# Neighbour rows of v copied in two blocks of 23 chunks instead of one of 47, with other numbers for the transfers in the plan and a new order

## The chip, the cores and the metric

The kernel runs on one core of one Trainium2 chip. Five instruction queues work beside each other: PE (TensorE, the matrix unit), DVE (VectorE), ACT (ScalarE), POOL (GpSimd) and SP (SyncE, which here only starts transfers). Each queue is executed strictly in order, and queues wait for each other by semaphores. Sixteen DMA engines move data between memory and the on-chip buffers. The metric is the device time of one execution in microseconds (us). Of each kernel several executions are timed; the median is quoted. One further execution is recorded by the hardware profiler, and all rows below come from such a recording.

## The reference

Chunked attention over 4 batches, 8 heads, 768 rows and head size 64. Each chunk of 32 queries sees its own 32 keys, 16 to the left, 8 to the right and 8 memory rows. Its output is laid out as 3072 tokens of 512 and goes into a noisy top-2 router over 8 experts, each of them two matrix products with a relu between.

```python
for c in range(S // 32):                      # 24 chunks
    l_start, r_end = max(0, c*32 - 16), min(S, c*32 + 32 + 8)
    k_full = concatenate([mem_k, k[:, :, l_start:r_end]], axis=2)
    v_full = concatenate([mem_v, v[:, :, l_start:r_end]], axis=2)
    a = softmax(q[:, :, c*32:c*32+32] @ k_full.T / sqrt(64))
    out[:, :, c*32:c*32+32] = a @ v_full
...
x = out.transpose(0, 2, 1, 3).reshape(3072, 512)
noisy = x @ w_gate + log1p(exp(x @ w_noise)) * noise
top2 = the two largest of each row of noisy, with their softmax as weights
for e in range(8):                            # w1[e] 512x1024, w2[e] 1024x512
    rows = tokens that chose e
    y[rows] += weight[rows] * (relu(x[rows] @ w1[e]) @ w2[e])
```

## The kernel before, in words

**Who decides the order.** The program isn't written in the order in which it runs. A planner (class `Planner`, L65 to L203) gets a list of operations. Each has a label, the engines it may run on with an assumed duration, the operations it depends on, the buffers it takes, a priority, and, where it starts a transfer, a pair `dma=(transfer, latency)`. `run` (L109) walks through time: of the operations that could start on an engine within 0.25 us of the earliest, it takes the one with the lowest priority number. It also picks the engine for operations that two could do. The instructions are then emitted in the order of the planned starts, and the hardware keeps to that order on each queue. Nothing of the plan's times is enforced on the chip; only the order and the choice of engine remain. Three things steer it: the durations, the table `SHIFT`, which adds to the priority of a label (or of its n-th operation, "label#n"), and `FETCH`, which describes pauses that the plan assumes for PE when it passes a multiple of 128 products (block, first edge, pause before a time, that time, pause behind it).

**Attention.** The work is cut into 16 pairs of heads (n = 0 to 15), 8 groups (g) of two pairs, and 4 batches (b) of four pairs. For each group the POOL queue loads q and k (`lq`, `lk`, L504, three buffers each) and v in two halves (`lv`, L513). A half of v holds two heads side by side as 48 chunks: for each chunk the 32 rows of the chunk itself stand on partitions 16 to 47 of the half's 64 partitions (three buffers, vg0 to vg2). Three kinds of small transfers on the SP queue fill the other partitions: the memory rows (`lm`, L524, out of `memv`, a part of the buffer XS that the experts use later), the 16 rows to the left (`spread`, L530, from the preceding chunk) and the 8 rows to the right (L531, from the following chunk). They copy within the buffer, over all 48 chunks of a half at once. The rows copied from one head into the other's edge are harmless: the scores there are masked.

Per pair there follow on PE, DVE and ACT: transposes of q and k (`tq`, `tk`, L551), their copies out (`eq`, `ek`, L367 and L369), scores (`sc`, L574 to L581), maximum (`mx`, L588), subtraction (`sb`, L604), exponential (`ex`, L607), transposes of the result (`tp`, L613) and their copy, the product with v (`pvo`, L627, 24 products; it needs `lm` and both halves' copies), reciprocal of the sums (`rc`, L631), multiplication into the row buffer of the batch (`ml`, L643), transposes of the rows (`tx`, L652).

**Ranking.** When a batch's four pairs are done, its 768 tokens are routed: logits (`lg`, L689), noise (`r1`, L695), choice of two experts (`r2`, L703 to L718, VectorE), running counts (`r3`, PE), a place in the experts' lists (`r3s` L745 and L747, `r6` L765 to L768), one-hot tables (`r8` L740, `r8a` L782), their product (`r9`, L789) and from it the indices by which the gathers fetch tokens (L798, L803, L816 in `tab`). The weights of the two experts come from `r4` (L755) and `r7` (L899 to L903). Tokens beyond a list's capacity are handled by `s0` to `s3` (L840 to L864). The SP queue writes each batch's finished rows to memory (`rows`, L909): batches 0 and 1 whole (row buffers xrow0 and xrow1), batches 2 and 3 (xrow2, xrow0 again) in two parts, `rows_x` as soon as the batch's last `ml` is done and `rows_g` after `r7`.

**Experts.** Indirect gathers on the POOL queue (L945) fetch 128 tokens each; PE turns them (L976), and they are copied into XS (`xev`, L367 and L369). Then each expert's first product (L1051), relu (L1061), second product (L1092), weighting and adding (L1101 to L1111), and scatter to the output (L1123). The weights w1 (L923) and w2 (L925) are loaded on the POOL queue too. The first gathers need only the lists of batches 0 to 2 (index buffer `gid_s`), the others those of all batches.

Of the kernel before, what the change touches and what calls it, by code (L numbers as in the profile page):

```python
# [22 lines left out]
FETCH = (128, 94, 6.9, 97.0, 3.2)  # L23
SHIFT = {
# [40 lines left out]
class Planner:  # L65
# [43 lines left out]
    def run(self):  # L109
        free, dma_free, sync_free, lanes, paced, products, busy = {}, 0.0, 0.0, [], 0.0, 0, 0.0  # L110
# [96 lines left out]
def kernel(  # L207
# [14 lines left out]
    nc = tc.nc  # L222
# [20 lines left out]
    OW = D + 2  # L243
# [253 lines left out]
    for g in range(NG):  # L497
# [11 lines left out]
        def v_load(o, hh, bv=bv, g=g, h0=h0, b=b):  # L509
# [7 lines left out]
                 prio=pr + 2 + 0.5 * hh, dma=(1.6, 1.6), tag="attn") for hh in range(2)]  # L517
# [8 lines left out]
        lm = op("lm", ("SP", 0.4), mem_rows, deps=[c_mv] + zd, after=lv, use=[bv], prio=pr + 3, dma=(0.3, 1.8), tag="attn")  # L526

        def spread(o, hh, bv=bv):
            vt = bv.t[64 * hh:64 * hh + 64, hh]
            nc.sync.dma_start(out=vt[:left_ctx, 1:], in_=vt[chunk:chunk + left_ctx, :2 * ncnk - 1])  # L530
            nc.sync.dma_start(out=vt[left_ctx + chunk:WIN, :2 * ncnk - 1], in_=vt[left_ctx:left_ctx + right_ctx, 1:])  # L531

        ln = [op("ln", ("SP", 0.3), lambda o, hh=hh, f=spread: f(o, hh), deps=[lv[hh]], after=[lm] if hh else [], use=[bv], prio=pr + 3 + 0.2 * (hh + 1), dma=(0.5, 1.8), tag="attn") for hh in range(2)]
        groups.append((bq, bk, bv, lq, lk, [lm] + ln))

    xrows = {}
# [726 lines left out]
```

## Time and profile before

| What | Value |
|---|---|
| timed runs | 338.48, 338.59 and 340.06 us |
| median | 338.59 us |
| the profiled execution's own time | 337.19 us |
| its span, first to last instruction | 335.70 us |
| mean granted TensorE clock in the span | 0.911 |
| data moved in the span | 43.56 MB in 56205 packets, 130 GB/s |

The execution falls into four parts. Attention runs until about 88 us, with loads on the DMA engines nearly all the time. From there to 126.5 us the end of attention and the ranking of batches 2 and 3 run, with VectorE the busiest engine. The experts run from 126.5 to 328.4 us, with PE busy almost without a gap. The last 7.3 us are the last tile's way to memory.

In the rows, a group of instructions is named by its engine, its line, and what it writes and reads; "[0.57 <-PE ps_o L627]" says that the engine had been idle for 0.57 us and what ended it. "SPq" and "POOLq" are the instructions that start a transfer on those queues.

### The profile page before, as it was taken

The numbers are of one execution on the slowest core, as the hardware profiler recorded it, in microseconds if no ns is written. First come the engines' busy times: TensorE is split into PE (matmuls) and PEld (weight loads), VectorE is DVE, ScalarE is ACT, GpSimd is POOL, SyncE is SP. The second block draws the span as 40 slices with busy tenths as digits, with TensorE's granted clock in tenths as the row PEclk, the third lists the DMA queues.
The fourth block names the chain that finished last, engine by engine and source line by source line (L and its number), as shares of the span: only waits on it lengthen the run. The fifth ranks groups of instructions, "written<-read, shape, count | busy, mean of one in ns | idle before, by whom it ended". The sixth has DMA issues, their size and how long they took to land.

```text
span 335.7 us, 7347 instructions
## 1 busy us (share of the span) xinstructions
PE 277.1 (83%) x2955; PEld 173.2 (52%) x2972; DVE 161.1 (48%) x370; ACT 146.0 (43%) x262; POOL 122.5 (36%) x177
## 2 busy tenths in 40 slices
PE   0683575767475659999999999999999999999991
PEld 0672464656354546664555755544544644744540
DVE  7683568897689886383243134043034023042141
ACT  7484765865494333762421621602701713704400
POOL 7771430332000494889752301232032032042062
PEclk9998769896795557999999999999999999999996
DMA  7999999999994249748999984884613612022022
GB/s 102 204 150 145 162 164 158 158 220 136 149 224 128 88 114 159 144 137 163 173 189 232 240 148 94 117 152 103 111 53 72 103 54 80 2 83 79 0 109 92
DMA packets 56205, 43.56 MB, mean 130 GB/s; under 512 B 29613, under 2 KB 49070, under 8 KB 56166
## 3 DMA queue, kind: packets, MB, share of 16 engines
q0 software_dynamic: 50096, 36.40, 83.7%
q1 hardware_dynamic: 5782, 6.57, 9.4%
q8 instruction: 24, 0.39, 0.5%
q14 instruction: 15, 0.12, 0.1%
q10 hardware_dynamic: 288, 0.07, 0.1%
HBM read 56.54 MB, written 10.85 MB: 201 GB/s over the span
## 4 chain that ended last, share of the span: by engine, by line
PE 55%; DMA 18%; DVE 9%; issue 8%; POOL 4%; ACT 2%; POOLq 2%; SPq 0%; DVEq 0%; ACTq 0%
PE ps_l L1092 19%; PE ps_l L1051 17%; DMA vg<-in_v_dram 11%; PE ps_g L1051 6%; PE ps_g L1092 5%; DMA vg<-vg 5%; POOL out_dram L1123 2%; PE ps_q L551 2%; DMA qn<-in_q_dram 2%; PE ps_o L627 1%; PE ps_l L976 1%; POOLq L1179 1%; DVE mx L588 1%; PE ps_g L652 1%; DVE xrow L643 1%
## 5 line engine op out<-in xcount | busy, mean ns | idle before, releaser
L1092 PE MATMUL ps_l<-w2l,ht 128*128 128x512 bf16 x341 | 78.2, 379 | 0.6
L1061 ACT ACTIVATE ht<-ps_l 128x384 bf16<-128x384 f32 (+2 forms) x106 | 47.7, 488 | 59.6 <-PE ps_l L1051 57.1
L1092 PEld LDWEIGHTS <-ht 128*128 128x128 bf16 x448 | 43.6, 98 | 51.1
L1123 POOL DMA_INDIRECT out_dram<-acc,oid x28 | 28.8, 1028 | 87.8 <-DVE acc L1111 82.9
L1111 DVE SCALAR_TENSOR_TENSOR acc<-ps_l,gates,acc 128x512 f32<-128x512 f32 x26 | 19.5, 751 | 63.9 <-PE ps_l L1092 61.0
L1051 PEld LDWEIGHTS <-w1t 128*128 128x128 bf16 x416 | 31.2, 99 | 19.2 <-issue 1.4
L1051 PE MATMUL ps_l<-XS,w1t 128*128 128x384 bf16 (+4 forms) x316 | 39.7, 284 | 0.0
L1051 PEld LDWEIGHTS <-w1l 128*128 128x128 bf16 x320 | 29.8, 98 | 18.8
L1061 ACT ACTIVATE ht<-ps_g 128x384 bf16<-128x384 f32 (+2 forms) x41 | 18.7, 490 | 46.7 <-PE ps_g L1051 46.5
L1051 PE MATMUL ps_l<-XS,w1l 128*128 128x256 bf16 (+3 forms) x240 | 38.8, 314 | 0.0
L627 PE MATMUL ps_o<-vg,PT 128*32 128x132 bf16 x384 | 12.5, 284 | 18.0 <-DMA vg<-vg 15.7
L367 ACT COPY kT<-ps_q 64x768 bf16<-64x768 bf16 x28 | 22.2, 792 | 10.8 <-PE ps_q L551 10.5
L513 POOL DMA_DIRECT2D vg<-in_v_dram x16 | 15.3, 960 | 25.2 <-PE ps_o L627 22.4
L1092 PE MATMUL ps_g<-w2l,ht 128*128 128x512 bf16 x91 | 21.9, 379 | 0.3
L551 PE MATMUL ps_q<-identb,qn 128*64 128x128 bf16 x192 | 11.3, 273 | 10.5 <-DMA qn<-in_q_dram 9.9
L945 POOL DMA_INDIRECT xl<-x_rows,gid x16 | 16.6, 1037 | 8.4 <-DMA w1t<-in_moe_w_dram 4.6
L1103 DVE TENSOR_SCALAR acc<-ps_l,gates 128x512 f32<-128x512 f32 x14 | 10.5, 751 | 18.5 <-PE ps_l L1092 15.3
L627 PEld LDWEIGHTS <-PT 128*32 128x32 bf16 x384 | 8.5, 122 | 20.4 <-issue 18.8
L607 ACT ACTIVATE P<-sd 128x768 bf16<-128x768 f32 x16 | 13.5, 845 | 6.3 <-DVE sd L604 6.1
L588 DVE TENSOR_REDUCE mx<-ps_s 128x12 f32<-128x768 f32 x16 | 15.2, 952 | 1.1 <-PE ps_s L581 1.0
L604 DVE TENSOR_TENSOR sd<-ps_s,mx 128x768 f32<-128x768 f32 x16 | 15.3, 956 | 0.8
L643 DVE TENSOR_TENSOR xrow<-ps_o,rec 128x768 bf16<-128x768 f32 x16 | 15.3, 957 | 0.5
(178 smaller groups left out, 369.6 us busy)
## 6 DMA issues: line engine op xcount, KB each, us to landing
w2l<-in_moe_w_dram POOLq DMA_DIRECT2D x8, 1024.0 KB, 9.5
w1t<-in_moe_w_dram POOLq DMA_DIRECT2D x4, 1024.0 KB, 20.9
w1l<-in_moe_w_dram POOLq DMA_DIRECT2D x4, 1024.0 KB, 8.3
kn<-in_k_dram POOLq DMA_DIRECT2D x8, 384.0 KB, 13.5
qn<-in_q_dram POOLq DMA_DIRECT2D x8, 384.0 KB, 11.6
vg<-in_v_dram POOLq DMA_DIRECT2D x16, 192.0 KB, 16.3
x_rows<-xrow SPq DMA_DIRECT2D x2, 792.0 KB
vg<-vg SPq DMA_DIRECT2D x16, 96.9 KB
```

What stands on the lines that cost most here:

```text
L367: A.copy(dst, src)
L513: G_.dma_start(out=vt[p0:p0 + chunk, hh, :, :D], in_=bass.AP(v.tensor, v.offset + hd * S * D, [[D, chunk], [chunk * D, 2 * ncnk], [1, D]]))
L551: P_.transpose(out=dst.t[64 * hh:64 * hh + 64, t * QP:(t + 1) * QP], in_=s[:, j + 2 * hh, t, :], identity=identb)
L588: mx = op("mx", ("DVE", 0.98), lambda o, bmx=bmx, bS=bS: V.tensor_reduce(out=bmx.t, in_=sv(bS), axis=AX, op=Alu.max), deps=[sc], alloc=[bm ...
L627: P_.matmul(out=pvw[32 * r:32 * r + 32, u // UB, u % UB], lhsT=PT[:, u, 32 * r:32 * r + 32], rhs=vt[:, :, ncnk * j + c], start=True, stop= ...
L643: V.tensor_tensor(out=x5, in0=ov(bO)[:, :, :, :, :D], in1=r5.to_broadcast([128, 2, UB, 2, D]), op=Alu.mult)
L945: G_.indirect_dma_start(out=bx.t[:n], out_offset=None, in_=src, in_offset=bass.IndirectOffsetOnAxis(ap=ids_[:n, c:c + 1], axis=0), bounds_ ...
L1051: P_.matmul(out=dst, lhsT=w1b[e].t[:, kp, f * 128:(f + 1) * 128], rhs=src, start=(kp == 0), stop=(kp == KP - 1), skip_group_check=True)
L1061: A.activation(out=dst, in_=s_, func=Act.Relu)
L1092: P_.matmul(out=gy.t, lhsT=ht.t[:, f, j, :], rhs=w2b[e].t[:, f, :], start=(f == 0), stop=(f == FB - 1))
L1111: V.scalar_tensor_tensor(out=ba.t, in0=gy.t, scalar=gate, in1=ba.t, op0=Alu.mult, op1=Alu.add)
L1123: G_.indirect_dma_start(out=out_part[nv], out_offset=bass.IndirectOffsetOnAxis(ap=oid[:, c:c + 1], axis=0), in_=ba.t, in_offset=None, boun ...
```

## The change

The copies of the neighbour rows are written over two heads with 23 chunks each, where they were written over 47 chunks that include the seam between the heads. The row of 48 x 66 elements is split as two of 24 x 66; a copy then has two blocks of 23 x 66 = 1518 elements per partition where it had one of 47 x 66 = 3102. The chunk that was copied across the seam isn't copied any more.

Beside it, numbers that only the planner uses change: what a transfer on SP costs (`lm` 0.4 to 1.3, `ln` 0.3 to 1.25, and 1.8 to 4.0 us until a neighbour copy has landed), a load of v (1.6 to 1.7), the pauses of `FETCH`, and the time at which engines and transfers start (1.1 to 4.75 us, formerly 0). The table `SHIFT` is another one. And the copies of gathered tokens into XS get one more dependency: on the last group's memory rows, which are read from a part of XS.

```diff
-FETCH = (128, 94, 6.9, 97.0, 3.2)
+FETCH = (128, 94, 6.6, 100.0, 3.2)
 SHIFT = {
-    "c_mv": 79.0, "c_ones": 19.7, "c_smallv": 124.2, "c_wg": 14.0, "ek": 14.6, "ek#23": 6.3, "ek#29": 11.1, "ep": 38.1, "ep#3": 23.7, "eq":
...
+    "ek": 19.8, "ek#17": -24.3, "ek#19": -51.3, "ep#1": -28.0, "eq#1": 19.5, "ex": 33.6, "ex#4": -21.4, "exx": 53.8, "exx#7": -17.1, "fo":
...
     def run(self):
-        free, dma_free, sync_free, lanes, paced, products, busy = {}, 0.0, 0.0, [], 0.0, 0, 0.0
+        free, dma_free, sync_free, lanes, paced, products, busy = dict(POOL=1.6, DVE=1.1, ACT=1.1, SP=1.1, PE=1.1), 4.75, 4.75, [], 0.0, 0, 0.0
...
         lv = [op("lv", ("POOL", 1.05), ...
-                 prio=pr + 2 + 0.5 * hh, dma=(1.6, 1.6), tag="attn") for hh in range(2)]
+                 prio=pr + 2 + 0.5 * hh, dma=(1.7, 1.6), tag="attn") for hh in range(2)]
...
-        lm = op("lm", ("SP", 0.4), mem_rows, deps=[c_mv] + zd, after=lv, use=[bv], prio=pr + 3, dma=(0.3, 1.8), tag="attn")
+        lm = op("lm", ("SP", 1.3), mem_rows, deps=[c_mv] + zd, after=lv, use=[bv], prio=pr + 3, dma=(0.3, 1.8), tag="attn")
 
         def spread(o, hh, bv=bv):
-            vt = bv.t[64 * hh:64 * hh + 64, hh]
-            nc.sync.dma_start(out=vt[:left_ctx, 1:], in_=vt[chunk:chunk + left_ctx, :2 * ncnk - 1])
-            nc.sync.dma_start(out=vt[left_ctx + chunk:WIN, :2 * ncnk - 1], in_=vt[left_ctx:left_ctx + right_ctx, 1:])
-
-        ln = [op("ln", ("SP", 0.3), lambda o, hh=hh, f=spread: f(o, hh), ..., dma=(0.5, 1.8), tag="attn") for hh in range(2)]
+            vt = bv.t[64 * hh:64 * hh + 64, hh].rearrange("p (j c) d -> p j (c d)", j=2)
+            nc.sync.dma_start(out=vt[:left_ctx, :, OW:], in_=vt[chunk:chunk + left_ctx, :, :-OW])
+            nc.sync.dma_start(out=vt[left_ctx + chunk:WIN, :, :-OW], in_=vt[left_ctx:left_ctx + right_ctx, :, OW:])
+
+        ln = [op("ln", ("SP", 1.25), lambda o, hh=hh, f=spread: f(o, hh), ..., dma=(0.5, 4.0), tag="attn") for hh in range(2)]
...
-            ev = op("xev", ..., xev, deps=[tt], use=[gx], prio=prio)
+            ev = op("xev", ..., xev, deps=[tt, groups[-1][5][0]], use=[gx], prio=prio)
```

The new order, at three places. The first is the SP queue behind the copies of group 5 (buffer vg2_100 until the row write, then group 6 in vg0_98); before, the row write of batch 0 (xrow0_78) stands between the two halves of group 4 (vg1_99).

Before:

```order
L530 DMA vg1_99<-vg1_99 16x3102
L531 DMA vg1_99<-vg1_99 8x3102
L909 DMA x_rows<-xrow0_78 128x6x264
L524 DMA vg2_100<-XS_77 8x3168 x2
L530 DMA vg1_99<-vg1_99 16x3102
L531 DMA vg1_99<-vg1_99 8x3102
L524 DMA vg0_98<-XS_77 8x3168 x2
```

Of the change:

```order
L530 DMA vg2_100<-vg2_100 16x2x1518
L531 DMA vg2_100<-vg2_100 8x2x1518
L909 DMA x_rows<-xrow0_78 128x6x264
L530 DMA vg0_98<-vg0_98 16x2x1518
L531 DMA vg0_98<-vg0_98 8x2x1518
```

The row write has moved behind all copies of groups 4 and 5, and directly ahead of those of group 6. The shape 16x2x1518 in place of 16x3102 is the copy in two blocks.

The second place is the end of the SP queue, where the copies of the last group (vg1_99) and the row writes of batches 1 (xrow1_79), 2 (xrow2_80) and 3 (xrow0_78 again) stand. Before:

```order
L524 DMA vg1_99<-XS_77 8x3168 x2
L909 DMA x_rows<-xrow1_79 128x6x264
L530 DMA vg1_99<-vg1_99 16x3102
L531 DMA vg1_99<-vg1_99 8x3102
L909 DMA x_rows<-xrow2_80 128x6x256
L530 DMA vg1_99<-vg1_99 16x3102
L531 DMA vg1_99<-vg1_99 8x3102
L909 DMA x_rows<-xrow2_80 128x6x8
```

Of the change:

```order
L524 DMA vg1_99<-XS_77 8x3168 x2
L909 DMA x_rows<-xrow2_80 128x6x256
L530 DMA vg1_99<-vg1_99 16x2x1518
L531 DMA vg1_99<-vg1_99 8x2x1518
L530 DMA vg1_99<-vg1_99 16x2x1518
L531 DMA vg1_99<-vg1_99 8x2x1518
L909 DMA x_rows<-xrow1_79 128x6x264
L909 DMA x_rows<-xrow2_80 128x6x8
```

Batch 2's rows now stand ahead of both halves of the last group's copies, and batch 1's behind them.

The third place is VectorE's queue around the last two multiplications of attention (L643, of pairs 14 and 15, into xrow0_78; the later one is pair 15's, "ml15"). The other names there belong to batch 2: pos, at and slot are its places, fl and fs part of them, ohl its one-hot table, gid_s the indices of the first gathers, tab the running list. Before:

```order
L765 TENSOR_TENSOR pos_2127<-ps_g0_84,pk_2041 128x168
L767 TENSOR_REDUCE at_2128<-pos_2127 128x6
L768 TENSOR_TENSOR slot_2129<-at_2128,fs_2051 128x6
L782 TENSOR_TENSOR ohl_158<-ramp_132,slot_2129 128x768
L631 RECIPROCAL rec0_113<-ps_o0_121 128x12
L643 TENSOR_TENSOR xrow0_78<-ps_o0_121,rec0_113 128x6x2x64
L803 SCALAR_TENSOR_TENSOR gid_s_162<-ps_g1_85,tab_161 128x28
L798 SCALAR_TENSOR_TENSOR gid_s_162<-ps_g1_85,tab_161 64x2x2
L798 SCALAR_TENSOR_TENSOR gid_s_162<-ps_g1_85,tab_161 64x2
L816 TENSOR_TENSOR tab_161<-ps_g1_85,tab_161 128x28
L631 RECIPROCAL rec1_114<-ps_o0_121 128x12
L643 TENSOR_TENSOR xrow0_78<-ps_o0_121,rec1_114 128x6x2x64
```

Of the change:

```order
L631 RECIPROCAL rec1_114<-ps_o0_121 128x12
L643 TENSOR_TENSOR xrow0_78<-ps_o0_121,rec1_114 128x6x2x64
L864 TENSOR_TENSOR tab_161<-ps_g1_85,tab_161 32x1
L745 TENSOR_TENSOR fl_2188<-pk_2084,flip_140 128x168
L747 TENSOR_REDUCE fs_2189<-fl_2188 128x6
L765 TENSOR_TENSOR pos_2199<-ps_g0_84,pk_2084 128x168
L767 TENSOR_REDUCE at_2200<-pos_2199 128x6
L768 TENSOR_TENSOR slot_2201<-at_2200,fs_2189 128x6
L782 TENSOR_TENSOR ohl_158<-ramp_132,slot_2201 128x768
L774 SCALAR_TENSOR_TENSOR base3_151<-ps_g0_84,smin_139 128x28
L840 TENSOR_REDUCE cap_2208<-pk_2084 128x6
L841 TENSOR_SCALAR cap_2208<-cap_2208 128x6
```

Batch 2's places, its one-hot table and its indices stand behind ml15, where they stood ahead of it; the indices gid_s follow three rows further on.

More of the change, by code (lines that the diff above doesn't have):

```diff
@@ L524, in mem_rows @@
                 nc.sync.dma_start(out=bv.t[64 * hh + WIN:64 * hh + CTX, hh], in_=memv[64 * hh + n_mem * g:64 * hh + n_mem * (g + 1)])
-        lm = op("lm", ("SP", 0.4), mem_rows, deps=[c_mv] + zd, after=lv, use=[bv], prio=pr + 3, dma=(0.3, 1.8), tag="attn")
+        lm = op("lm", ("SP", 1.3), mem_rows, deps=[c_mv] + zd, after=lv, use=[bv], prio=pr + 3, dma=(0.3, 1.8), tag="attn")
         def spread(o, hh, bv=bv):
-            vt = bv.t[64 * hh:64 * hh + 64, hh]
-            nc.sync.dma_start(out=vt[:left_ctx, 1:], in_=vt[chunk:chunk + left_ctx, :2 * ncnk - 1])
-            nc.sync.dma_start(out=vt[left_ctx + chunk:WIN, :2 * ncnk - 1], in_=vt[left_ctx:left_ctx + right_ctx, 1:])
-        ln = [op("ln", ("SP", 0.3), lambda o, hh=hh, f=spread: f(o, hh), deps=[lv[hh]], after=[lm] if hh else [], use=[bv], prio=pr + 3 + 0.2 * (hh + 1), dma=(0.5, 1.8), tag="attn") for hh in range(2)]
+            vt = bv.t[64 * hh:64 * hh + 64, hh].rearrange("p (j c) d -> p j (c d)", j=2)
+            nc.sync.dma_start(out=vt[:left_ctx, :, OW:], in_=vt[chunk:chunk + left_ctx, :, :-OW])
+            nc.sync.dma_start(out=vt[left_ctx + chunk:WIN, :, :-OW], in_=vt[left_ctx:left_ctx + right_ctx, :, OW:])
+        ln = [op("ln", ("SP", 1.25), lambda o, hh=hh, f=spread: f(o, hh), deps=[lv[hh]], after=[lm] if hh else [], use=[bv], prio=pr + 3 + 0.2 * (hh + 1), dma=(0.5, 4.0), tag="attn") for hh in range(2)]
         groups.append((bq, bk, bv, lq, lk, [lm] + ln))
@@ L985, in turn_ops @@
             w = KP * m * 128
-            ev = op("xev", DA(0.2 + w / 1900, 0.2 + w / 1250), xev, deps=[tt], use=[gx], prio=prio)
+            ev = op("xev", DA(0.2 + w / 1900, 0.2 + w / 1250), xev, deps=[tt, groups[-1][5][0]], use=[gx], prio=prio)
             for ps, _ in units:
@@ L1003, in turn_ops @@
             d_ = 0.4 if half and len(ps) > 1 else 0.2
-            ev = op("xev_a" if half == 0 else "xev", ("ACT", 0.2 + w / 1250) if half == 0 else DA(d_ + w / 1900, d_ + w / 1250), xev, deps=[tt], use=[gx], prio=prio)
+            ev = op("xev_a" if half == 0 else "xev", ("ACT", 0.2 + w / 1250) if half == 0 else DA(d_ + w / 1900, d_ + w / 1250), xev, deps=[tt, groups[-1][5][0]], use=[gx], prio=prio)
             for p in ps:
```

26 rows, old and new, of the table SHIFT are left out of this document.

## The prediction

> **What bounds the kernel now.** I read the page first (busy shares, the granted clock, the DMA share), then a table of stages cut where the chain of waits changes its nature, then the chain itself.
>
> ```profile
> PE 277.1 (83%) x2955; PEld 173.2 (52%) x2972; DVE 161.1 (48%) x370; ACT 146.0 (43%) x262; POOL 122.5 (36%) x177
> PEclk9998769896795557999999999999999999999996
> DMA  7999999999994249748999984884613612022022
> ```
>
> DMA is at 9 tenths from the second slice to the twelfth (8.4 to about 100 us), and the TensorE clock drops in exactly that part. PE's 83% is therefore an average of two different kernels. The stage table tells them apart (columns: stretch, length, busy us of PE, PEld, DVE, ACT, POOL, granted clock, DMA share, GB/s).
>
> ```profile
> 0.00:31.50 31.50, 14.44 (x290) 12.34 (x290) 20.93 (x43) 20.29 (x20) 21.10 (x60) 0.98 1.70 152
> 31.50:88.50 57.00, 37.18 (x903) 29.58 (x903) 41.74 (x86) 36.26 (x52) 15.00 (x18) 0.80 2.05 163
> 88.50:126.50 38.00, 24.97 (x495) 20.86 (x495) 31.75 (x98) 18.62 (x30) 12.40 (x16) 0.63 0.71 139
> 126.50:150.50 24.00, 23.53 (x251) 16.11 (x251) 14.56 (x62) 14.05 (x50) 16.86 (x21) 0.94 0.76 151
> 150.50:328.40 177.90, 176.95 (x1019) 94.33 (x1034) 51.41 (x81) 56.73 (x111) 55.82 (x62) 1.00 0.55 113
> 328.40:335.70 7.30, 0.00 (x0) 0.00 (x0) 0.75 (x1) 0.00 (x0) 1.28 (x2) 0.65 0.20 69
> ```
>
> From 126.5 to 328.4 us, the expert stage, PE is busy 200.48 of 201.90 us: only 1.42 us can be won there. The last 7.3 us are the last scatter. So nearly all that this change can win or lose lies before 126.5 us, in attention and ranking. The chain there:
>
> ```profile
> 27.02 20.94 DMA vg<-in_v_dram
> 47.98 0.54 SPq L530
> 48.57 8.86 DMA vg<-vg
> 57.57 0.85 PE ps_o L627 x24
> ...
> 80.77 0.54 SPq L530
> 81.36 7.04 DMA vg<-vg
> 88.53 0.85 PE ps_o L627 x24
> ```
>
> Up to 88.5 us the end is set by loads of v, then by the neighbour copies (7.04 and 8.86 us from issue to release), then by the product with v (L627). The load at 27.02 takes 20.94 us because it stands behind the loads of q and k issued before it. Behind 88.5 us VectorE takes over (columns: stretch, length, busy us, clock, DMA share, GB/s):
>
> ```profile
> 88.50:93.80 5.30, 3.01 (x4) 0.70 1.62 164
> 93.80:104.00 10.20, 9.62 (x24) 0.90 1.04 219
> 104.00:114.80 10.80, 9.24 (x27) 0.50 0.16 44
> 114.80:126.50 11.70, 9.87 (x46) 0.50 0.52 146
> ```
>
> 28.73 busy of 32.7 us: from 93.8 us on what counts is in which order VectorE's queue stands, and whether the last v is there in time.
>
> **The copies.** Count of DMAs, partitions and source: unchanged, 32 copies. Bytes fall by one chunk of 48 per row and direction (3102 to 3036 elements, 2%), and the runs double, from one to two per row. The trace has no copy of two runs. Its nearest rows are the two landings above, 7.04 and 8.86 us for the same bytes: their difference, 1.82 us, bounds what a copy may gain or lose by its form; I take 0, since the bytes are nearly the same and the copies' time is mostly waiting beside the loads. The Trainium skill ("DMA: Bandwidth & Descriptors", section "Queues, rings and completion order") says that each DMA engine goes round the queues with work, one packet at a time. If the two runs are two packets, each copy waits for one more packet of the loads; no row here shows a packet's turn. By that rule the sum could only rise, within the same 1.82 us.
>
> **The plan's numbers** (durations of copies, start times, prefetch) cost nothing themselves: they choose the order. The added dependency of the late copies into XS on the last memory rows is no wait: on the SP queue those rows stand ahead of the last copies, which are issued by 99.78 us, and XS is first written at 122.78 us (both rows below).
>
> **Loads of q, k, v.** The POOL queue now builds the identity first and then starts q before k. The sixteen v loads and sixteen q and k loads stay on one queue, and the last two v loads still have all others and one w1 load ahead of them. While that queue is never empty, their landing depends on the amount, not on the order: 0. The SP queue, though, changes what stands beside them.
>
> ```profile
> 63.62 0.43 SPq L909 DMA_DIRECT2D x_rows<-xrow  x1
> 82.68 0.64 SPq L531 DMA_DIRECT2D vg<-vg  x1
> 88.03 0.39 SPq L909 DMA_DIRECT2D x_rows<-xrow  x1
> 98.40 0.39 SPq L909 DMA_DIRECT2D x_rows<-xrow  x1
> 99.78 0.65 SPq L531 DMA_DIRECT2D vg<-vg  x1
> x_rows<-xrow SPq DMA_DIRECT2D x2, 792.0 KB
> ```
>
> A row write of 792 KB at the 163 GB/s of that stretch is 5.0 us of the DMA engines. Batch 0's (63.62) moves behind the copies of group 5 and so in front of those of group 6; batch 1's (88.03) moves behind all copies; batch 2's (98.40) moves from between the copies of the last group to in front of both. One write less ahead of the last group, one more ahead of group 6: I take 0, with ends of -5.0 and +5.0 us. Group 6 has room: its copies, issued by 82.68, land by 91.5 even at 8.86, and its product ran at 96.75 us.
>
> **VectorE's end** is the term that I can count. Call S the start of the last product's multiply (ml15).
>
> ```profile
> 95.07 0.95 DVE L369 COPY qT<-ps_q 128x768 bf16<-128x768 bf16 x1
> 103.92 0.49 DVE L745 TENSOR_TENSOR fl<-pk,flip 128x168 bf16<-128x168 bf16 x1
> 104.69 0.19 DVE L755 TENSOR_REDUCE m<-nl 128x6 f32<-128x48 f32 x1
> 109.38 0.32 DVE L765 TENSOR_TENSOR pos<-ps_g,pk 128x168 f32<-128x168 f32 x1
> 110.30 0.56 DVE L782 TENSOR_TENSOR ohl<-ramp,slot 128x768 f16<-128x768 f16 x1
> 111.43 0.23 DVE L631 RECIPROCAL rec<-ps_o 128x12 f32<-128x12 f32 x1 [0.57 <-PE ps_o L627]
> 112.58 0.18 DVE L803 SCALAR_TENSOR_TENSOR gid_s<-ps_g,tab 128x28 int32<-128x28 f32 x1
> 113.61 0.23 DVE L631 RECIPROCAL rec<-ps_o 128x12 f32<-128x12 f32 x1 [0.36 <-PE ps_o L627]
> 113.88 0.96 DVE L643 TENSOR_TENSOR xrow<-ps_o,rec 128x768 bf16<-128x768 f32 x1
> 118.39 0.21 DVE L703 TENSOR_TENSOR nn<-ns,nz_all 128x48 f32<-128x48 f32 x1
> ```
>
> Batch 2's placing (fl to its successor, 0.77; pos to the end of ohl, 1.48; the gather indices from 112.58 to the wait before 113.61, 0.67) goes from ahead of ml15 to behind it, and a copy of qT (0.86 to its successor) goes to ScalarE: 3.8 us less ahead of S, and the two waits of 0.57 and 0.36 for products stand where that work stood. S moves from 113.88 to between 109.2 (waits gone) and 110.1. The data allow about the same: the last copies, issued at 99.78, land at 106.8 to 108.6; two products of 0.85 and a reciprocal of 0.23 follow, so S is 108.8 to 110.6. I take 109.2.
>
> What is late next: the first gather, which now needs batch 2's placing behind ml15.
>
> ```profile
> 113.24 1.18 POOL L945 DMA_INDIRECT xl<-x_rows,gid_s  x1 [8.93 <-DVE tab L816]
> 122.78 1.84 ACT L367 COPY XS<-ps_l 128x512 bf16<-128x512 bf16 x4 [1.08 <-PE ps_l L976]
> 126.53 3.03 PE L1051 MATMUL ps_l<-XS,w1t 128*128 128x384 bf16 x16
> 96.75 0.53 PE L627 MATMUL ps_o<-vg,PT 128*32 128x132 bf16 x24
> ```
>
> In the new order: S, ml15 0.96, fl and fs 0.77, pos to the start of ohl 0.92, then ohl, the table product and the indices, which before took 2.94 (110.30 to 113.24) with PE occupied by a product in between, and at least 1.9 without (0.56, 0.67 and about 0.7 of product and handover, an estimate from those rows); I take 2.1. First gather: 109.2 + 4.75 = 113.95. From the first gather to the last turned copy is 11.38 us (113.24 to 124.62), so the experts start at 125.3 instead of 126.53: **1.2 us earlier**. Batch 3's ranking, 8.14 us from 118.39 to 126.53, starts once VectorE has done batch 2's placing and the overflow of two batches, about 7 us behind S, that is at 116.2, and ends at 124.3: ahead of the gathers, so it doesn't set the start. If PE no longer hides a stall there, each microsecond shows, as there is nothing else for it to do.
>
> **Sum.** Copies 0 (-1.8 to +1.8), what stands beside the loads 0 (-5.0 to +5.0), start of the experts -1.2 (ends by S and the 2.1: -2.1 to +0.9), expert stage 0 (-1.4, its whole idle time, to about +1.4, as much again where a weight now waits). The profiled execution took 337.19 us with a span of 335.70; 337.19 - 1.2 = 336.0. The median of the three runs, 338.59, lies 1.40 above it, so on that scale: **337.4 us**.
>
> **Rivals.**
> - The loads win: with batch 1's rows out of the way the last v lands up to 5 us earlier, and VectorE, which idles 2.29 of 5.3 us before 93.8, uses it. It can use some 3 us, as in the next 10.2 us it has only 0.58 idle. S at 106.2, experts at 122.3: 334.4. For it: the chain's waits for copies. Against it: batch 2's rows take the freed place.
> - Nothing moves: gathers and ranking end at the same time as before, 338.6. For it: the gathers' chain of 11.38 us is untouched.
> - Slower, by the SP queue: batch 2's rows stand ahead of both halves of the last group's copies, and batch 0's ahead of group 6's. If these rows are issued just before the copies, the last ones land up to 5 us later, at 111.8 to 113.6, and PE, in order, holds the last products and everything behind them. It decides from a landing of 110 us on (S beyond 111.8 less two products), then microsecond for microsecond; halfway, at 112.5, the experts start 2.5 us later than before: 341.1. The same holds for a copy that loses its 1.82 us.
> - That the blocks copy no faster is contained in the forecast, which gives them 0.
>
> **Chances.** Forecast (336 to 338.4) 0.38, the loads win 0.20, nothing moves 0.19, slower 0.23. The measurement can tell 0.5%, 1.7 us, from no change: faster means under 336.9, slower over 340.3. The forecast's case falls half under 336.9. Faster 0.20 + 0.19 = 0.39, same 0.19 + 0.19 = 0.38, slower 0.23. The range runs from the loads' rival with its whole 5 us used (332.4) to the queue's rival at its latest landing, 113.6, which is 3.6 us later (342.2); beyond lie only cases in which several terms meet, some 2 in 10.
>
> **What would show it.** Right: L627's last product near 108.5, ml15 at 109, a first gather at 114, a first L1051 near 125.3, and an unchanged 202 us from there to the last product. The copies' landing, 7 to 9 us in the chain, tells of their form. Wrong: a wait of PE at L627 for vg of over 3 us behind 94 us (the queue's rival), a first L1051 ahead of 123.5 (the loads' rival), or gaps of PE of over 2 us within the expert stage, by gathers queued behind w1 and w2 loads, which I gave 0.

## The result and the profile after

| | Median us | Runs | Ratio to before, 95% interval |
|---|---|---|---|
| before | 337.66 | 20 (334.38 to 340.34) | |
| the change | 333.87 | 20 (330.41 to 561.66) | 0.9874 (0.9844 to 0.9903) |

The change is faster by 1.3% (0.97% to 1.56%): 4.3 us of 337.66. The forecast was 1.2 us. The ratio leaves disturbed runs out, eight of the change's twenty, and so says a little more than the medians of all runs, which are 3.8 us apart. The profiled execution of the change took 335.39 us, 1.5 us above its median, at a granted clock of 0.891; where the size of a gain in the profile matters, I read that of the second experiment, whose order is the same.

The page of the change first, then its stage table with the columns of before (stretch, length, busy us of PE, PEld, DVE, ACT, POOL, granted clock, DMA share, GB/s).

```profile
PE 278.9 (84%) x2972; PEld 173.6 (52%) x2972; DVE 155.8 (47%) x360; ACT 152.1 (46%) x271; POOL 123.3 (37%) x178
PEclk9977597768965658999999999999999999999997
DMA  7999999979994429999899610899704521012022
```

```profile
31.50:88.50 57.00, 41.33 (x975) 33.53 (x979) 39.56 (x78) 40.45 (x57) 14.68 (x18) 0.72 1.75 163
88.50:126.50 38.00, 22.54 (x399) 17.62 (x392) 30.68 (x111) 15.83 (x28) 12.50 (x17) 0.62 0.80 134
126.50:150.50 24.00, 23.36 (x237) 15.33 (x236) 9.45 (x41) 16.29 (x55) 20.53 (x26) 0.97 1.08 196
```

The shares of busy time hardly tell the two kernels apart. What differs is where work lies: from 31.5 to 88.5 us PE has done 41.33 us (before 37.18) and ACT 40.45 (36.26), in the same 57 us and with the same 163 GB/s. Not all of that is attention moved forward: in the stage behind, PE has only 2.4 us less and ACT 2.8. PE's clock was lower (0.72 for 0.80), and over the whole run ACT has nine instructions more and VectorE ten less. VectorE, the bound of the next stage, keeps 9.45 us of work behind 126.5, where it kept 14.56; that belongs to the new order of the experts, for with their old order (e12, below) it is 14.66 again. The sub-stages of VectorE (stretch, length, busy us, clock, DMA share, GB/s) and the chain of waits of the change say when:

```profile
88.50:93.80 5.30, 4.57 (x15) 1.00 2.64 141
93.80:104.00 10.20, 7.45 (x18) 0.50 0.93 247
104.00:114.80 10.80, 8.07 (x35) 0.66 0.33 98
```

```profile
82.53 12.39 DMA vg<-in_v_dram
94.94 0.63 SPq L530
95.61 7.57 DMA vg<-vg
103.27 0.85 PE ps_o L627 x24
...
106.56 0.81 PE ps_o L627 x24
107.39 0.24 DVE rec L631
```

Before, VectorE was packed from 93.8 us on (0.58 idle in 10.2); now it is 2.75 idle there, and the chain runs through the last load of v, its copy and the last products. The last group's copies were issued at 98.88 and 99.78 before; now at 94.94 and 95.61, and the last product starts at 106.56. The chain has changed its nature: up to the last product it is the transfers again, not VectorE's queue.

### The profile page after: what moved, and what is told of

Same layout as the page of the kernel before. It is cut to its first block, busy times and chain, and to the rows that moved or that the text cites. A ratio compares the mean times of both kernels' runs of the same rounds, so it can differ in the third digit from the quotient of the medians.

```text
span 333.9 us, 7356 instructions
## 1 busy us (share of the span) xinstructions
PE 278.9 (84%) x2972; PEld 173.6 (52%) x2972; DVE 155.8 (47%) x360; ACT 152.1 (46%) x271; POOL 123.3 (37%) x178
## 4 chain that ended last, share of the span: by engine, by line
PE 50%; DMA 22%; issue 14%; DVE 6%; POOL 5%; POOLq 1%; SPq 0%; ACT 0%; DVEq 0%
PE ps_l L1092 20%; PE ps_l L1051 17%; DMA vg<-in_v_dram 8%; PE ps_g L1051 6%; PE ps_g L1092 5%; DMA qn<-in_q_dram 5%; DMA vg<-vg 4%; DMA xl<-x_rows,gid_b 2%; DMA kn<-in_k_dram 2%; POOL out_dram L1123 2%; PE ps_l L976 1%; POOL vg L513 1%; DVE gates L957 1%; POOL qn L504 1%; PE ps_o L627 0%
## 5 line engine op out<-in xcount | busy, mean ns | idle before, releaser
L1061 ACT ACTIVATE ht<-ps_l 128x384 bf16<-128x384 f32 (+2 forms) x110 | 48.3, 470 | 82.6 <-PE ps_l L1051 82.0
L1092 PE MATMUL ps_l<-w2l,ht 128*128 128x512 bf16 x352 | 79.6, 379 | 0.0
L1111 DVE SCALAR_TENSOR_TENSOR acc<-ps_l,gates,acc 128x512 f32<-128x512 f32 x24 | 18.0, 751 | 66.6 <-PE ps_l L1092 65.7
L1051 PE MATMUL ps_l<-XS,w1t 128*128 128x384 bf16 (+4 forms) x316 | 41.9, 285 | 0.0
L1051 PEld LDWEIGHTS <-w1t 128*128 128x128 bf16 x416 | 31.4, 100 | 19.6 <-issue 1.9
L1051 PEld LDWEIGHTS <-w1l 128*128 128x128 bf16 x320 | 29.8, 98 | 18.9
L1051 PE MATMUL ps_l<-XS,w1l 128*128 128x384 bf16 (+3 forms) x236 | 38.6, 313 | 0.0
L1061 ACT ACTIVATE ht<-ps_g 128x384 bf16<-128x384 f32 (+2 forms) x36 | 15.8, 466 | 24.8 <-PE ps_g L1051 24.8
L945 POOL DMA_INDIRECT xl<-x_rows,gid x16 | 16.8, 1048 | 15.9 <-PE ps_g L976 8.3
L957 DVE COPY gates<-xl 64x8 f32<-64x8 f32 (+1 forms) x40 | 10.8, 271 | 21.1 <-DMA xl<-x_rows,gid 11.6
L367 ACT COPY PT<-ps_g 128x768 bf16<-128x768 bf16 x15 | 12.0, 798 | 13.2 <-PE ps_g L613 7.5
L367 ACT COPY qT<-ps_q 128x768 bf16<-128x768 bf16 x16 | 12.8, 798 | 9.0 <-PE ps_q L551 7.1
L613 PE MATMUL ps_g<-identb,P 128*128 128x128 bf16 x96 | 10.8, 267 | 6.8 <-ACT P L607 5.7
L1051 PE MATMUL ps_g<-XS,w1l 128*128 128x512 bf16 (+3 forms) x84 | 15.7, 321 | 0.0
## 6 DMA issues: line engine op xcount, KB each, us to landing
w2l<-in_moe_w_dram POOLq DMA_DIRECT2D x8, 1024.0 KB, 10.2
```

The source lines that it names most:

```text
L367: A.copy(dst, src)
L945: G_.indirect_dma_start(out=bx.t[:n], out_offset=None, in_=src, in_offset=bass.IndirectOffsetOnAxis(ap=ids_[:n, c:c + 1], axis=0), bounds_ ...
L957: V.tensor_copy(gates[rows, cc, :], bx.t[rows, XC:].bitcast(F32))
L1051: P_.matmul(out=dst, lhsT=w1b[e].t[:, kp, f * 128:(f + 1) * 128], rhs=src, start=(kp == 0), stop=(kp == KP - 1), skip_group_check=True)
L1061: A.activation(out=dst, in_=s_, func=Act.Relu)
L1092: P_.matmul(out=gy.t, lhsT=ht.t[:, f, j, :], rhs=w2b[e].t[:, f, :], start=(f == 0), stop=(f == FB - 1))
```

## The experiments

All ran as the kernel before did, with its runs on the same chip in between. The chip was one for e1 to e3, another for e4 to e11 and a third for e12, so that across them the ratios compare better than the times. Four numbers are read from each trace: S (start of ml15, the last multiplication, L643), the start of the first gather (L945), of the first expert product (L1051), and the span. They are times of one profile each, and a microsecond or two between two rows are no finding by themselves: the same order of attention and ranking, profiled four times (the change, e2, e3, e12), gave a first L1051 at 124.04, 122.65, 123.96 and 125.08.

| Kernel | Ratio | 95% interval | S | gather | L1051 | span |
|---|---|---|---|---|---|---|
| before | 1 | | 113.88 | 113.24 | 126.53 | 335.7 |
| the change | 0.9874 | 0.9844–0.9903 | 107.66 | 112.25 | 124.04 | 333.9 |
| e1 copies in two blocks alone | 1.0012 | 0.9985–1.0039 | 114.40 | 113.76 | 127.05 | 336.2 |
| e2 plan and order alone | 0.9899 | 0.9858–0.9940 | 106.27 | 110.87 | 122.65 | 331.6 |
| e3 the change again | 0.9884 | 0.9849–0.9919 | 107.59 | 112.17 | 123.96 | 333.8 |
| e4 before, row writes late | 0.9932 | 0.9900–0.9964 | 110.92 | 110.03 | 123.79 | 334.8 |
| e5 before, placing behind ml15 | 1.0072 | 1.0035–1.0109 | 112.82 | 116.98 | 128.48 | 339.7 |
| e6 change, w1 behind the last v | 0.9832 | 0.9783–0.9881 | 109.89 | 114.48 | 126.29 | 335.3 |
| e7 change, placing ahead of ml15 | 0.9875 | 0.9822–0.9928 | 110.20 | 110.44 | 124.86 | 334.1 |
| e8 e4 and e5 together | 1.0035 | 1.0000–1.0070 | 110.07 | 114.24 | 125.75 | 335.8 |
| e9 e4 and the new order of loads | 0.9919 | 0.9883–0.9955 | 112.75 | 111.87 | 125.62 | 335.6 |
| e10 change, gathered rows turned earlier | 0.9843 | 0.9777–0.9909 | 107.09 | 111.68 | 122.04 | 331.6 |
| e11 e7, and experts ahead of the ranking | 0.9936 | 0.9893–0.9979 | 108.26 | 108.49 | 118.92 | 332.8 |
| e12 change, experts in the old order | 0.9928 | 0.9896–0.9959 | 108.71 | 113.30 | 125.08 | 334.8 |

From e4 on the edits move named operations in the list that the planner has made, and the program is emitted in exactly that list's order. In the diffs, `move([a, b], c)` is short for "a and b go right behind c" and `ahead` for "right ahead of c"; names are those of the section on the kernel, "#n" being the n-th of its kind. `ln#11` is the second half of group 5's copies, `ln#14` and `ln#15` are the two halves of the last group's.

### The blocks alone, the order alone, both (e1, e2, e3)

```diff
 # e1, on the kernel before: only the form of the copies
+            vt = bv.t[64 * hh:64 * hh + 64, hh].rearrange("p (j c) d -> p j (c d)", j=2)
+            nc.sync.dma_start(out=vt[:left_ctx, :, OW:], in_=vt[chunk:chunk + left_ctx, :, :-OW])
...
 # e2, on the change: only the form of the copies, back
-            vt = bv.t[64 * hh:64 * hh + 64, hh].rearrange("p (j c) d -> p j (c d)", j=2)
+            vt = bv.t[64 * hh:64 * hh + 64, hh]
+            nc.sync.dma_start(out=vt[:left_ctx, 1:], in_=vt[chunk:chunk + left_ctx, :2 * ncnk - 1])
...
```

> The order and the plan's numbers of before, with only the copies written in two blocks. Theory ORDER (the gain is the new order): ratio to before 1.00 within 0.4%, last v load landing near 98.5 us as before. Theory BLOCKS (the copies in two blocks take less of the DMA engines: their packets took 27 us of 16 engines' span less a half in the page's queue table, 8.2% for 9.4%): ratio 0.990 to 0.995, last v load landing 2 to 4 us earlier, S (start of the last L643) near 110. Theory PACKETS (twice the packets, each waits its turn behind the loads): slower, ratio 1.003 to 1.01.

> The order and the plan's numbers of the change, with the copies of before in one block of 47 chunks. Theory ORDER: ratio to before 0.987 as the change, S near 107.7 us. Theory BLOCKS: ratio 0.992 to 0.997, and the last v load lands 2 to 4 us later than the change's 94.9. Theory PACKETS: faster than the change, ratio 0.98.

> The change unaltered, on the same chip as the two above, for its ratio here (0.987 expected) and a second profile: S near 107.7, the first gather near 112.3, the first L1051 near 124.0, and from there 202 us to the last product, if the first profile is typical. If the missing gain (3.8 us in the medians, 1.8 us between the two profiles) lies in this one profile, its first L1051 comes near 122.

Measured: 1.0012 (0.9985 to 1.0039) for the blocks, 0.9899 for the order, 0.9884 for both. The change is its order; the copies in two blocks give nothing that can be told from no change. The trace shows that they did become something else. Here is the SP queue of the page, before and in e1 (packets, MB, share of 16 engines):

```profile
q1 hardware_dynamic: 5782, 6.57, 9.4%
```

```profile
q1 hardware_dynamic: 6166, 6.52, 9.2%
```

384 packets more are 24 for each of 16 halves, that is one more for each of its 16 + 8 partitions. The chain of e1 has the copy that before took 7.04 us:

```profile
80.95 0.62 SPq L530
81.62 6.76 DMA vg<-vg
88.51 0.85 PE ps_o L627 x24
```

6.76 us with two runs beside 7.04 with one. What did grow is the instruction that starts the copy: 0.62 us, where the prediction's chain has 0.54 for it. The rule of the Trainium skill that the prediction weighed ("DMA: Bandwidth & Descriptors", section "Queues, rings and completion order": engines go round the queues, one packet at a time) would have let the time only rise if each run were a turn of its own; twice the runs cost no measurable time here.

### Row writes late (e4)

```diff
 # on the kernel before
+move(["rows#0"], "ln#11")
+move(["rows#1"], "ln#15")
+move(["rows_x_s#0"], ahead="ln#14")
```

> The kernel before, with only the three row writes moved to the places that they have in the change: batch 0's behind the copies of group 5, batch 1's behind all copies, batch 2's ahead of both halves of the last group. In the change the loads of v of group 5 land at 72.9 us for 80.8 before, those of group 7 at 94.9 for 98.5. Theory ROWS (the row writes, 5 us of the DMA engines each, held the loads up): group 5 lands at 76 to 78, group 7 at 94 to 96 here; the time gains little, since VectorE's order holds S near 113: ratio to before 0.994 to 1.000. Theory LOADS (the loads come earlier because POOL issues them in another order and waits less): group 5 still lands at 80 or later, group 7 at 97.5 or later, ratio 1.000.

Measured: 0.9932 (0.9900 to 0.9964), 2.3 us, more than half of what the change brings, from three instructions in other places on the SP queue. The bytes are the same. What moved is which of them are ahead of loads that somebody waits for. First the SP queue of e4 (start us, us, queue, line, operation):

```profile
75.94 0.54 SPq L530 DMA_DIRECT2D vg<-vg  x1
...
78.69 0.54 SPq L530 DMA_DIRECT2D vg<-vg  x1
...
80.01 0.43 SPq L909 DMA_DIRECT2D x_rows<-xrow  x1
...
96.42 0.54 SPq L530 DMA_DIRECT2D vg<-vg  x1
```

Before, the copies of group 5, which wait for its loads, were issued at 79.41 and 80.77: the two halves are 3.5 and 2.1 us earlier. Some 0.8 us of that is no effect of the edit: group 5's loads themselves were issued at 61.60 for 62.41, ahead of anything that was moved. Of the three writes only batch 0's stood ahead of these copies (issued at 63.62). Where its bytes went shows in a table of eight-microsecond windows (stretch, length, clock, DMA share, GB/s), before and e4:

```profile
64.00:72.00 8.00, 1.00 1.57 203
72.00:80.00 8.00, 0.67 2.43 160
80.00:88.00 8.00, 0.91 1.85 142
```

```profile
64.00:72.00 8.00, 0.79 2.00 145
72.00:80.00 8.00, 0.83 2.20 142
80.00:88.00 8.00, 0.96 1.69 215
```

73 GB/s over 8 us, 0.58 MB of the 0.81 MB of a row write (792 KB of 1024 bytes), appear in the third window; 58 GB/s have left the first. In the first window the write ran beside the loads of group 5, in the third it runs beside a load of w1 and those of the last group, whose copies are nevertheless issued earlier than before. The next place where it shows is PE, at the product with v of pair 10, before and in e4:

```profile
88.53 0.85 PE L627 MATMUL ps_o<-vg,PT 128*32 128x132 bf16 x24 [3.54 <-DMA vg<-vg]
```

```profile
85.63 0.53 PE L627 MATMUL ps_o<-vg,PT 128*32 128x132 bf16 x24 [1.32 <-DVE ge L900]
```

The wait of 3.54 us for a copy is gone, the product is 2.9 us earlier, and so is S (2.96), which the theory ROWS had left near 113, and the first L1051 (2.74). The last group's own copies are only 2.5 us earlier (98.88 to 96.42), less than group 5's first half: taking batch 1's rows from ahead of them and putting batch 2's there comes out at nothing more. Each write by itself wasn't tried, so that it is batch 0's rests on the order of these rows. Nor does the whole lead last in this profile: in the expert stage PE waits 1.21 us for a relu (L1061), and a product that started at 134.67 before starts at 134.21 here, 0.46 us earlier. The spans of the two profiles are 0.9 us apart; the ratio of many runs is worth 2.3.

### Batch 2's placing behind ml15 (e5, e7, e8)

The term that the prediction counted, alone on the kernel before (e5), taken back out of the change (e7), and with the row writes (e8):

```diff
 # e5, on the kernel before (e8: with the three moves of e4)
+move(["r3_s#0"], "tp#15")
+move(["r3s_s#0", "r6_s#0", "r8a_s#0", "nb_s#0", "r9_s#0", "tab_s#0", "idl#0", "tab2#0", "gather_a#0"], "ml#15")
 # e7, on the change
+move(["r3_s#0"], ahead="pvo#14")
+move(["r3s_s#0"], ahead="rc#14")
+move(["r6_s#0", "r8a_s#0", "nb_s#0", "r9_s#0", "tab_s#0", "idl#0", "tab2#0"], "r7_s#0")
+move(["gather_a#0"], "ml#15")
```

> The kernel before, with only batch 2's running counts, placing, one-hot table and gather indices moved behind the last multiply (ml15) as in the change: the term that the prediction counted. Theory FORECAST: S (start of ml15) falls from 113.9 to about 109.2 to 110, first gather near 114, first L1051 about 1.2 us earlier, ratio to before 0.9965. Theory DATA (the last v, landing at 98.5 as before, holds S): S not under 111, the first gather near 116, the first L1051 later than before, ratio 1.000 to 1.006.

> The change, with only batch 2's running counts, placing, table and gather indices moved back ahead of the last multiply, as they stood before. S about 2 us later (109.7), first gather about 3 us earlier (109). Theory GATHER (the first gather starts the chain to the experts, 11.4 us long): first L1051 near 120.5, ratio to before 0.977. Theory RANKING (batch 3's ranking on VectorE, behind S, starts them, since PE takes its products in order): first L1051 stays at 123.5 to 125, ratio 0.985 to 0.990.

> The kernel before with both edits that were tried alone: the three row writes late (alone 0.9932) and batch 2's placing behind ml15 (alone 1.0072). Theory SUM (each costs what it cost alone): ratio 1.000, first L1051 near 126. Theory TOGETHER (the placing pays as the prediction counted it, once the last v is early): ratio 0.985 to 0.989, S near 107.7, as in the change, since nothing else would then be missing. Between them, at 0.993, the placing would be free once the v is early.

Measured: alone it costs 0.7% (1.0072), undone in the change it makes no difference (0.9875), and with the row writes it eats their gain (1.0035; the product of the two ratios is 1.0004). VectorE's rows of e5:

```profile
110.70 0.23 DVE L631 RECIPROCAL rec<-ps_o 128x12 f32<-128x12 f32 x1 [1.99 <-PE ps_o L627]
...
112.55 0.23 DVE L631 RECIPROCAL rec<-ps_o 128x12 f32<-128x12 f32 x1 [0.63 <-PE ps_o L627]
112.82 0.96 DVE L643 TENSOR_TENSOR xrow<-ps_o,rec 128x768 bf16<-128x768 f32 x1
```

With the placing out of the way VectorE waits 1.99 and 0.63 us for the products: S gains 1.06 us, and the first gather, which stands 4.16 us behind S, loses 3.74. Taking work from ahead of S pays only as far as the products are there. In e7 the opposite: the first gather is 1.8 us earlier than in the change, and the experts are not earlier. PE's rows of e7:

```profile
118.47 0.32 PE L731 MATMUL ps_l<-pk,upper 128*128 128x168 bf16 x1 [1.85 <-DVE pk L718]
...
122.26 0.46 PE L789 MATMUL ps_l<-ohv,ohl 128*128 128x28 f16 x6 [1.96 <-DVE ohl L782]
...
124.86 1.65 PE L1051 MATMUL ps_g<-XS,w1t 128*128 128x384 bf16 x8
```

Between the gathers and the first L1051 PE stands at batch 3's ranking: 1.85 us for its choice (pk), 1.96 for its one-hot table (ohl). The change shows the same, with its places in order:

```profile
117.15 0.32 PE L731 MATMUL ps_l<-pk,upper 128*128 128x168 bf16 x1 [1.86 <-DVE pk L718]
...
120.96 0.46 PE L789 MATMUL ps_l<-ohv,ohl 128*128 128x28 f16 x6 [1.99 <-DVE ohl L782]
122.24 0.17 PE L831 MATMUL ps_l<-ov,upper 128*128 128x6 bf16 x1 [0.82 <-DVE ov L842]
...
122.46 0.91 PE L976 MATMUL ps_g<-identb,xl 128*128 128x128 bf16 x8
123.51 0.44 PE L861 MATMUL ps_l<-tnum,ohs 128*32 128x1 f16 x6
124.04 1.65 PE L1051 MATMUL ps_g<-XS,w1t 128*128 128x384 bf16 x8
```

The second turning of gathered rows (L976) waits for nothing of its own: it stands behind the ranking's L831 in PE's queue.

### Experts ahead of the ranking (e10, e11)

If the ranking holds the start, gathered rows can be turned ahead of it. e10 does so with the second group of rows, e11 goes on from e7 and puts the first expert product too ahead of batch 3's tables.

```diff
 # e10, on the change
+move(["tt_a#1", "xev_a#2", "xev_a#3"], "gather_a#4")
+move(["fo_a#3"], ahead="s3_l#0")
 # e11, on e7, its first gathers behind ml#15
+move(["tt_a#0", "xev_a#0", "xev_a#1"], "s3_s#0")
+move(["tt_a#1", "xev_a#2", "xev_a#3", "fo_a#3"], "r3_l#0")
```

> The change, with three things of the first experts moved up on PE and ScalarE: the second turn of gathered tokens (L976) ahead of the product of batch 3's table (L789), its copies into XS behind it, and the first expert product (L1051) ahead of batch 3's last spare product (L861). Theory ORDER OF PE (the experts start behind batch 3's ranking only because PE takes its products in order): first L1051 near 122.5 for 124.0, ratio to before 0.982 to 0.985. Theory ELSEWHERE (the time comes back as a wait in the expert stage, for the gathers that need batch 3's lists): ratio 0.987 to 0.989 as the change, with a gap of PE of over 1 us behind 130 us.

> The change, with batch 2's placing and indices ahead of the last multiply (alone 0.9875, no gain, since batch 3's ranking stood ahead of the experts on PE), and now both turns of gathered tokens and the first expert product moved up as well: the first turn ahead of batch 3's running counts, the second and the first L1051 right behind them. Theory ORDER OF PE: first L1051 near 121.3, ratio 0.978 to 0.982. Theory ELSEWHERE: 0.986 to 0.989, with gaps of PE of over 1 us in the expert stage, or with a first L1051 later than 123.

PE's rows of e10, then of e11:

```profile
119.72 0.39 PE L976 MATMUL ps_l<-identb,xl 64*128 64x64 bf16 x4 [0.86 <-DMA xl<-x_rows,gid_s]
...
122.04 1.65 PE L1051 MATMUL ps_l<-XS,w1t 128*128 128x384 bf16 x8
```

```profile
118.92 1.65 PE L1051 MATMUL ps_l<-XS,w1t 128*128 128x384 bf16 x8 [0.67 <-ACT XS L367]
121.68 0.46 PE L789 MATMUL ps_g<-ohv,ohl 128*128 128x28 f16 x6 [1.11 <-DVE ohl L782]
...
123.74 0.44 PE L861 MATMUL ps_g<-tnum,ohs 128*32 128x1 f16 x6 [0.91 <-DVE ohs L850]
124.11 3.17 PE L1051 MATMUL ps_l<-XS,w1t 128*128 128x384 bf16 x16
```

In e10 the gathered rows are there 8.0 us behind the first gather (111.68 to 119.72), and PE now does wait for them, 0.86 us. By the same 8.0 us (an estimate: one profile's distance put into another) they were there at 120.3 in the change, and were turned at 122.46. So in the change the gathers' chain ends some 2 us ahead of the ranking's: the two are near to balance, and this would explain why neither e5's mechanism nor e7's shows in it. e11 starts the experts 5.1 us earlier than the change and then gives most of it back: PE waits for the same ranking behind the first eight matmuls (1.11 and 0.91 us in these rows), and the next ones run at 124.11, where the change starts its first (124.04). What was won is the 1.65 us of those eight. 0.9936, which neither theory had, is above the change's 0.9874 with overlapping intervals; e10's 0.9843 is what ORDER OF PE had, but its interval (0.9777 to 0.9909) covers the change and the other theory too. Neither is shown to differ from the change.

### Loads, weights, experts (e9, e6, e12)

```diff
 # e9, on e4: the POOL queue's first operations in the change's sequence (identity first, q ahead of k)
+for at, o in zip(sorted(seq.index(o) for o in loads), loads): seq[at] = o
 # e6, on the change: the first load of w1 behind the last load of v
+move(["o10#0"], "lv#15")
 # e12, on the change: the expert stage's operations in the sequence and on the engines of before
+for at, (o, eng) in zip(sorted(seq.index(o) for o, _ in late), late): seq[at], o.eng = o, eng
```

> The kernel before with the three row writes late (alone 0.9932), and with the loads of q, k and v on the POOL queue in the change's sequence as well, among them both loads of v of group 1 ahead of the next q. Theory LOADS (the rest of the change's gain, about 0.5%, is the order of the loads): ratio 0.986 to 0.990, the copies of the last group issued near 92.6 and 94.9 as in the change, for 94.95 and 96.4 with the rows alone. Theory AMOUNT (while the queue is never empty only the amount counts, as the prediction had it): 0.993 as with the rows alone, the copies issued as there.

> The change, with only the load of the first w1 (1 MB) moved from ahead of to behind the last two loads of v on the POOL queue. The last v should then land near 89 for 94.9 us. Theory DATA (in the new order the last v's copies hold S): S falls from 107.7 to about 105.5, where VectorE's 2.7 us of waits between 94 and 107.6 are used up, and the first L1051 as much: ratio to before 0.980 to 0.983. Theory VECTORE (its queue alone holds S): S and ratio as in the change, 0.987.

> The change, with the expert stage (step-1 gathers, weight loads behind the first two w1, turns, products, relus, scatters, and the engines chosen for them) in the sequence of the kernel before; loads, copies, attention, ranking and the first gathers stay as in the change. Of the change's 1.2%, the row writes alone gave 0.7%, the placing and the loads gave nothing. Theory ATTENTION (the rest is the joint order of attention and ranking): ratio 0.986 to 0.990 as the change, first L1051 near 123.5. Theory EXPERTS (the rest is the new order of the expert stage): ratio 0.992 to 0.994, and from the first L1051 to the last product about 203 us for 202.

e9: 0.9919 beside e4's 0.9932; the order of the loads on their own queue is not measurable. e6: 0.9832 (0.9783 to 0.9881) is near what the theory DATA had, but overlaps the change's interval too, so the place of this load decides nothing that I can show. Its profile is of its slowest run (336.81 us, median 333.21): S is later there and not earlier, and it shows something else, told at the end. e12: 0.9928 (0.9896 to 0.9959) lies above the change's 0.9874 with intervals that just overlap, and e3, the change again, reaches to 0.9919. It points to 0.4 to 0.5% for the new order of the experts, but its trace doesn't show it where it should be: behind the first L1051 it has 209.7 us (334.8 less 125.08), before has 209.2 and the change 209.9. This profile too is of the slowest run (336.31 us, median 334.50); its first L1051 is 1.0 us later than in the change, though nothing ahead of it was edited. Whether there is such a half per cent, and what it is, stays open.

## Why the prediction was right, and where it was not

**Direction and range** held: 333.87 lies between 332.4 and 342.2, though 3.5 below the 337.4 that was named: the gain was more than three times the forecast one, and the range held because it had been drawn out to the rivals. About half of the gain (e4) came by the mechanism of the rival "the loads win" (334.4), with another write than the one it named. Of that rival's sign, a first L1051 ahead of 123.5, the profiles say both: 124.04 in the change, 122.65 in e2.

**The copies: 0.** Held, by e1 (1.0012) and by e2 and e3, which differ by their form alone.

**What stands beside the loads: 0 (-5.0 to +5.0).** This term was mis-sized: it measured -0.7%, 2.3 us (e4). "One write less ahead of the last group, one more ahead of group 6: I take 0" left out that batch 0's write, in leaving its old place, also leaves the way of group 5's loads; as far as the rows of e4 tell, the gain lies there. Group 6 had the room that the prediction gave it; group 5 had none, as the chain of before said: its last copy (81.36, 7.04 us) was the last thing that PE waited for ahead of 88.53. I counted writes per group and not what each one stood in front of.

**VectorE's end.** S moved to 107.66 where 109.2 was forecast. But the reason given, work taken from ahead of S, is wrong in sign if it is alone (e5: +0.7%) and without effect on the time in the change (e7). The forecast let it take full effect, with products that allowed an S of 108.8 to 110.6; in e5 they were late, by 1.99 and 0.63 us. S came forward because the products did: by 2.96 us with the row writes alone (e4). The placing has a part in S too (put back ahead, in e7, it makes S 110.20), but not one that reaches the time. The distance from S to the first gather, 4.75 forecast, was 4.59: that part of the count held.

**The start of the experts: 125.3, by the gathers.** It was 124.04 (122.65 in e2), by the ranking. The step that failed is "ahead of the gathers, so it doesn't set the start". Its number was good: batch 3's ranking forecast to end at 124.3, ended at 123.95 (L861, 123.51 + 0.44). The comparison was not: the gathers' 11.38 us included turned rows that stood behind the ranking in PE's queue. The first L1051 of before was 13.3 us behind its first gather, 1.9 more than the 11.38, and the prediction didn't ask what filled these. PE's rows of before show it:

```profile
121.71 1.78 PE L976 MATMUL ps_l<-identb,xl 128*128 128x128 bf16 x16
125.01 0.17 PE L831 MATMUL ps_l<-ov,upper 128*128 128x6 bf16 x1 [1.52 <-DVE ov L842]
...
126.16 0.44 PE L861 MATMUL ps_g<-tnum,ohs 128*32 128x1 f16 x6 [0.22 <-DVE ohs L850]
126.53 0.82 PE L1051 MATMUL ps_l<-XS,w1t 128*128 128x384 bf16 x2
```

Behind the turned rows PE waited for batch 3's ranking already then; the ranking set the start before the change too.

**The expert stage: 0.** Nearly: from the first L1051 to the end before took 209.2 us, the change 209.9, e2 209.0. The gain is all ahead of it: in e2 3.9 us at the first L1051 (126.53 to 122.65) and 4.1 in the span (335.7 to 331.6).

**The rival "slower, by the SP queue".** Batch 2's rows were issued at 90.20, the last copies behind them by 95.61, and their product ran at 103.27, not at 111 or later. PE waited 2.12 us for them, less than the 3 us that the prediction named as this rival's sign. What batch 2's rows cost at this place wasn't tried apart.

**A reading of the page** was wrong, though no term rests on it. The clock doesn't drop "in exactly that part" where DMA is at 9 tenths: it is at 9 tenths beside DMA at 9 in the slices 2 and 3, and lowest, at 5, in the slices 13 to 15 (100.7 to 125.9 us), where DMA is at 4, 2 and 4.

**What isn't settled.** Of 4.3 us, 2.3 come from the row writes. The placing (e7) and the order of loads (e9) are not shown to give any of the rest; their intervals are some 0.4 to 0.5% wide to each side. The expert order is a candidate by its ratio alone (e12), and the other moves of VectorE's, PE's and ScalarE's work in attention weren't tried apart.

## What to carry to other kernels

A large write that nobody waits for can cost by what it stands in front of (2.3 us in e4, for three of them): for each place that it leaves and each that it takes, name the load that is in flight there and who waits for it, and compare with the chain of waits, not with the count of bytes. When an engine's queue is in order, what starts a stage is the last instruction ahead of it in that queue, even one that the stage doesn't need; subtract the forecast chain from the time that was measured before, and if it leaves a remainder, find out what fills it. Moving the stage ahead of that instruction wins little where the queue must wait for it right behind (e11). And work taken from ahead of an end that two engines share pays only up to the point where the other engine's result is there.

## What the runs showed of the hardware

In e6 the copies of the last group were issued from 93.06 us on, and PE got them at 105.79. Here are the rows of the POOL queue, the SP queue and PE of e6:

```profile
85.79 0.77 POOL L923 DMA_DIRECT2D w1t<-in_moe_w_dram  x1
...
86.98 0.79 POOL L923 DMA_DIRECT2D w1t<-in_moe_w_dram  x1
```

```profile
95.27 0.70 SPq L531 DMA_DIRECT2D vg<-vg  x1
```

```profile
105.79 0.85 PE L627 MATMUL ps_o<-vg,PT 128*32 128x132 bf16 x24 [3.70 <-DMA vg<-vg]
```

From the end of the last issue to the product it is 9.8 us, beside two loads of 1 MB on the other queue; by the same count the change has 7.0 us (95.61 + 0.70 to 103.27), and the other profiles of its order (e2, e3, e10, e12) 6.3 to 6.8. As far as this one profile tells, a small transfer on its own queue isn't served ahead of a large one on another, while its own number of runs had no measurable effect (e1). And the timing of one recorded execution moves by 2.4 us at the same place for the same order (122.65 to 125.08), twice the term that the prediction counted: only ratios over many runs told e5 from e7.
